# Spacing the shuffles of two blocks' quotients, and moving four small VectorE instructions behind the features of block 1

## The chip, the cores and the metric

The kernel runs on one core of a Trainium2 chip. The core has five engines that work side by side, each through its own instruction queue in order: TensorE (PE in the profile; PEld is its loading of weights), VectorE (DVE), ScalarE (ACT), GpSimd (POOL) and SyncE (SP), which here only issues DMAs. The metric is the device time of the whole launch in microseconds; lower is better. Engines wait for each other through semaphores. SBUF is the on-chip memory that all engines read and write, PSUM the eight banks into which TensorE multiplies.

## The reference

One input `x` of 2048 tokens by 640 numbers is normalized, and two layers run on the normalized tokens side by side: linear attention with a learned feature map (32 heads of 20 numbers), and an MLP of 1728 hidden numbers with a normalization of its own.

```python
xn = _layernorm(x)
# attention
q, k, v = split(xn @ wqkv)                       # 32 heads of 20
phi(p) = concat(softmax(p @ w_phi), softmax(-p @ w_phi))
kv  = einsum("hsf,hsd->hfd", phi(k), v);  z = sum_s phi(k)
o   = einsum("hqf,hfd->hqd", phi(q), kv) / (einsum("hqf,hf->hq", phi(q), z) + 1e-6)
A   = o @ wo
# MLP
y   = _layernorm(xn)
B   = gelu(y @ w1 + b1) @ w2 + b2
out = x + A + B
```

Both normalizations start from the same mean and variance of a token, so the kernel computes two inverse deviations for each token from one variance: `ry`, by which the MLP's input is scaled, and `rs_all`, by which the exponentials of the attention's features are scaled.

## The kernel before

All matmuls are float32 made of parts: a number is split into a high and a low half (ScalarE writes the high half, VectorE or GpSimd subtracts it from the number to get the low one), and a product takes three matmuls (high by high, high by low, low by high; lines 70 to 72). The tokens are in four blocks of 512, b = 0 to 3. The stages, in order of time:

- To about 213 us: normalization, and the MLP of blocks 0 and 1. The hidden layer is cut in 14 pieces of 128, taken in pairs g = 0 to 6. `passes(g, b, ws)` multiplies two pieces, applies gelu, and multiplies back; VectorE adds each of the five results to `acc[b]` (L329 for g = 0, L331 later).
- To about 431 us: the attention's projections, softmax features, and the sums over keys, one tile of 128 tokens after the other.
- To about 640 us: the MLP of blocks 2 and 3. For g = 1 to 5 `cross` makes the first products of both blocks together, and `second` the products back (accumulated by L342). Between them runs `attend`, the attention's second half, for the four blocks in turn.
- To the end: the attention's output times `wo`, added to `acc`.

**Ticks.** After each product of three matmuls the program calls `mlp.tick()`. It first issues what is due at that tick (`mlp.after(n, step)` puts a step n ticks ahead), then takes one step of the generator `mlp.beside`. So work of the other engines is put between TensorE's products by hand. On VectorE, ScalarE and GpSimd the order of instructions is the order of the program (from L1357 on, and up to L872, by `manual_schedule`; TensorE's from L516 to the end); the order of SP's queue is not written by hand but made by a planner, which puts a DMA where it takes it to be ready.

**The start.** `stats` (L132) yields between its parts; its last part (L160 to L162) is a reciprocal of 128 x n numbers and a product of the same size, which give `rs_all`. Three such generators stand for tokens 0 to 255 (`s01`), 256 to 511 (`s23`) and 512 to 1023 (`s47`). `next_y` (L653) is the `beside` of the first two passes: it runs what is left of gelu for block 0 (`zs`), splits the last weights (`parts`), and makes the MLP's input of block 1 in five chunks: GpSimd subtracts the mean (L679), VectorE multiplies (L681), ScalarE writes the high half (L683), VectorE the low one (L685). L671 turns the feature weights once.

**The attention's second half.** `Attention.groups` loads the features `e` eleven times for a block, splits them (`first`: ScalarE L1206, GpSimd L1207) and multiplies (`second`: L1213, L1214, into one of two banks); ScalarE moves one half of the result (L1223), and two ticks later VectorE adds the other (L1227) into the block's tile `ob`. There are two such tiles: block 2 uses that of block 0, block 3 that of block 1 (L1165). A group takes four ticks; a block takes 50.

When a block's groups are through, its `quotients` (L1234) run: denominators go to DRAM and come back with 128 of them in a row (`dt`), VectorE inverts them (L1246), they go to DRAM again, and five DMAs bring them to `rx`. Then, for each of five chunks, VectorE spreads the inverses over the partitions (`stream_shuffle`, L1262), GpSimd multiplies (L1264), and for blocks 0 and 1 a DMA stores the chunk to `ob_dram` (L1266), since another block takes the tile. `load_ob` (L1386) brings blocks 0 and 1 back before the last stage, with one DMA of 1280 KB each (L1388). `attend` (L1313) steps the groups and all quotients that have begun, one step of each for a tick.

Of the kernel before, what the change touches and what calls it, by code (L numbers as in the profile page):

```python
# [46 lines left out]
def f(ap):  # L47
    return ap.bitcast(F32)
# [3 lines left out]
def tile_kernel(ctx: ExitStack, tc: tile.TileContext, x, xT, wkT, wqT, wv, wphi, wo, w1, b1, w2, b2,  # L52
# [79 lines left out]
    def stats(ts, xp, xbs, turned=False, eng=nc.vector):  # L132

        t0, n = ts[0], len(ts)
        st = xp.tile([P, n, 2, 6], F32, name="st", bufs=2)
        for i, (t, xb) in enumerate(zip(ts, xbs)):
            for h in range(2):
                nc.vector.bn_stats(st[:, i, h, :], xb[:, h * 320:(h + 1) * 320])  # L138
            nc.vector.bn_aggr(mv[:, t, :], st[:, i, :, :])
            yield  # L140


        ts = slice(t0, t0 + n)
        q = xp.tile([P, 2, n], F32, name="q", bufs=2)
        eng.tensor_scalar(q[:, 1, :], mv[:, ts, 1], 0.25 * (1 + EPS), 0.25 * EPS * EPS, op0=ALU.mult, op1=ALU.add)
        eng.tensor_scalar(q[:, 0, :], mv[:, ts, 1], 0.25, 0.25 * EPS, op0=ALU.mult, op1=ALU.add)
        yield

        sr = xp.tile([P, 2, n], F32, name="sr", bufs=2)
        rr = xp.tile([P, 2, n], F32, name="rr", bufs=2)  # L150
        nc.scalar.activation(sr, q, AF.Sqrt)
        nc.vector.reciprocal(rr, sr)
        nc.vector.tensor_tensor(rr, rr, q, op=ALU.mult)
        if turned:
            nc.vector.scalar_tensor_tensor(sr, sr, -1.0, rr, op0=ALU.mult, op1=ALU.subtract)
        else:
            nc.vector.tensor_tensor(sr, sr, rr, op=ALU.add)
        nc.vector.reciprocal(ry[:, ts], sr[:, 1, :])
        yield
        ra = xp.tile([P, n], F32, name="ra", bufs=2)  # L160
        nc.vector.reciprocal(ra, sr[:, 0, :])
        nc.vector.tensor_tensor(rs_all[:, ts], sr[:, 1, :], ra, op=ALU.mult)  # L162
# [41 lines left out]
    def load_rows(b, i=5):  # L204

        mr = mtile(i)
        loads[b] = nc.sync.dma_start(mr.rearrange("p a t -> p (a t)"),
                          (r_dram[1][0] if b == 1 else r_dram[2][b - 2]).rearrange("r t -> (r t)").unsqueeze(0).to_broadcast([P, 8 * P])).ins
        return mr
# [309 lines left out]
    def finish(p):  # L519
        for _ in p:  # L520
            pass
# [46 lines left out]
    s01, s23, s47 = (stats(range(a, b), xp, xbs, b < 8, nc.gpsimd if a == 2 else nc.vector) for a, b, xbs in ((0, 2, x0[:2]), (2, 4, x0[2:]), (4, 8, x1)))  # L568

    def step(gen, n):  # L570
        for _ in range(n):
            next(gen, None)
# [56 lines left out]
    def raws(batch):  # L629
        ts = []  # L630
        for us in batch:
            raw = fp.tile([P, D], F32, name="raw")
            for n, g, u, nu, i in by_group(us):
                r, kk = g * G6, G6 if g < 5 else 2 * DH
                for j, one in enumerate(n):
                    with tc.issue_after(loads[1]) :
                        nc.sync.dma_start(raw[j * kk:(j + 1) * kk, u * P:(u + nu) * P],
                                          {"k": wkT, "q": wqT}[one][r:r + kk, i.start * P:i.stop * P])
            ts.append(raw)
        return ts  # L640
# [12 lines left out]
    def next_y():  # L653

        for _ in range(3):
            yield
        next(rows1)
        for z in zs[:2]:
            z()
        finish(rows1)  # L660
        mr = load_rows(1)
        first_raws.extend(raws(jobs[0]))
        for z in zs[2:]:
            z()
        for c in range(2, 4):
            parts[c][1]()
        for st in (s23, s47):
            step(st, 1)
        for _ in range(4):
            yield  # L670
        nc.vector.tensor_tensor(wpt[:, :, :, 1:], wpt[:, :, :, 1:], wpt[:, :, :, 0:1].to_broadcast([G6, 6, 6, DF]), op=ALU.subtract)  # L671
        for _ in range(9):
            yield
        xcs = {}
        for n in range(2 * KC + 5):
            c, i = divmod(n, 2)
            if i == 0 and c < KC:
                xcs[c] = xp.tile([P, D], F32, name="xb")[:, :512]
                nc.gpsimd.tensor_tensor(xcs[c], acc[1][:, c], mr[:, 0], op=ALU.subtract)  # L679
            if i == 0 and 0 <= (d := c - 1) < KC:  # L680
                nc.vector.tensor_tensor(xcs[d], xcs[d], mr[:, 1], op=ALU.mult)  # L681
            if i == 1 and 0 <= (d := c - 1) < KC:
                nc.scalar.activation(y[1][0][:, d], xcs[d], AF.Copy)  # L683
            if i == 0 and 0 <= (d := c - 2) < KC:
                nc.vector.tensor_tensor(y[1][1][:, d], xcs[d], f(y[1][0][:, d]), op=ALU.subtract)  # L685
            yield

    mlp.beside = next_y()
    p10 = mlp.passes(1, 0, [wc[2], wc[3]])
    next(p10)  # L690
# [470 lines left out]
    class Attention:  # L1161
# [72 lines left out]
        def quotients(self):  # L1234

            den, rden = d_dram[self.b]
            ob, parts = self.ob, [(slice(0, 20), "(q c) t -> q c t", 4), (slice(20, 30), "(q c) t -> q c t", 2)]
            for i, (r, form, q) in enumerate(parts):
                nc.sync.dma_start(den[r].rearrange(form, q=q), ob[30 + i::128 // q])
            dt = ep.tile([P, P], F32, name="dt")  # L1240
            nc.sync.dma_start(dt, den.rearrange("h (q t) -> (h q) t", q=4))
            for i in range(2):
                nc.sync.dma_start(ob[30 + i::32], o_dram[self.b].rearrange("(q i c) t -> i q c t", i=2, c=KC)[i])
            for i in range(13):
                yield
            nc.vector.reciprocal(dt, dt)  # L1246
            nc.sync.dma_start(rden.rearrange("h (q t) -> (h q) t", q=4), dt)
            for i in range(6):
                yield

            nc.sync.dma_start(rx[0::32], rden[0:20].rearrange(parts[0][1], q=4))
            yield
            for o in (0, 32):
                nc.sync.dma_start(rx[o + 1::64], rden[20:30].rearrange(parts[1][1], q=2))
                yield
                nc.sync.dma_start(rx[o + 2::64], rden[30:32].unsqueeze(1).to_broadcast([2, KC, 512]))
                yield
            for i in range(12):
                yield
            for c in range(KC + 1):  # L1260
                if c < KC:
                    nc.vector.stream_shuffle(rx[:, c, :], rx[:, c, :], SPREAD)  # L1262
                if c:
                    nc.gpsimd.tensor_tensor(ob[:, c - 1, :], ob[:, c - 1, :], rx[:, c - 1, :], op=ALU.mult)  # L1264
                    if self.b < 2:
                        nc.sync.dma_start(ob_dram[self.b][:, c - 1], ob[:, c - 1])  # L1266
                for i in range(3):
                    yield

        def split(self, c, eng):  # L1270
# [137 lines left out]
    step = 0  # L1408
# [79 lines left out]
```

## Time and profile before

| | us |
|---|---|
| median of 3 runs | 712.24 |
| lowest and highest of them | 711.95, 714.44 |
| the profiled execution | 711.95 |
| its span in the profile | 710.2 |
| TensorE busy | 703.4 |
| VectorE busy | 514.5 |
| GpSimd busy | 421.7 |
| ScalarE busy | 341.5 |

The profile is of one execution. Its span runs from the first to the last instruction; the launch takes 1.75 us more. A row of the timeline has start, duration (both in us), engine, line, operation, what is written and read, shapes, and a count; in brackets the engine's idle time before it and who ended it. Rows of SPq are issues of DMAs: their time is that of the issue, not of the transfer. A row of the waits has who waited, for whom, the sum in us, how often, and the longest. A row of the stretches has the stretch, its length, then busy time (and count) of PE, PEld, DVE, ACT and POOL, TensorE's granted clock, the share of the DMA engines and GB/s.

### The profile page before, as it was taken

What the parts mean: (1) busy time and instruction counts of PE and PEld (TensorE: products, weight loads), DVE (VectorE), ACT (ScalarE), POOL (GpSimd) and SP (SyncE); (2) the same over time, 40 slices, a digit from 0 to 9 for tenths busy, and PEclk for the clock granted to TensorE, in tenths of its full rate; (3) what the DMA queues carried; (4) which work ended last, traced back from release to release, by engine and by line L of the source; (5) the groups of instructions that cost most, each with busy time, mean ns of one, the idle gap of its engine ahead of it and who ended that gap; (6) DMA issues with size and microseconds to landing.
All of it is one profiled execution on the core that took longest, in us unless ns stands there. A gap on an engine that the chain in (4) does not pass through costs nothing.

```text
span 710.2 us, 9748 instructions
## 1 busy us (share of the span) xinstructions
PE 703.4 (99%) x3381; PEld 591.9 (83%) x3381; DVE 514.5 (72%) x819; ACT 341.5 (48%) x563; POOL 421.7 (59%) x362
## 2 busy tenths in 40 slices
PE   9999999999999999999999999999999999999998
PEld 7788888888888888888888888888888878888886
DVE  7977755978754788788888878757769686884622
ACT  6534554344334545544544547367666766450100
POOL 3621314577245997898787879458679887540400
PEclk9999999999999999999999999999999999999999
DMA  9823643485621227336401608963455568436222
GB/s 327 271 90 114 191 119 97 156 264 176 214 105 74 93 75 238 78 105 200 104 0 25 167 0 335 226 209 112 124 163 155 169 188 315 147 125 214 86 78 74
DMA packets 65767, 106.56 MB, mean 150 GB/s; under 512 B 7462, under 2 KB 31814, under 8 KB 63838
## 3 DMA queue, kind: packets, MB, share of 16 engines
q1 hardware_dynamic: 65414, 105.93, 46.7%
q8 instruction: 26, 0.43, 0.3%
q14 instruction: 23, 0.19, 0.1%
q10 hardware_dynamic: 304, 0.01, 0.0%
HBM read 71.37 MB, written 34.55 MB: 149 GB/s over the span
## 4 chain that ended last, share of the span: by engine, by line
PE 94%; DVE 3%; DMA 1%; ACT 1%; issue 0%; SPq 0%; DVEq 0%
PE bank L905 28%; PE bank L70 19%; PE bank L72 18%; PE bank L71 18%; PE bank L975 3%; PE bank L646 2%; PE bank L1213 1%; PE bank L1214 1%; DMA xb<-in_x 1%; DVE st L138 1%; DMA r<-sr 1%; PE bank L326 1%; PE bank L308 1%; PE bank L327 1%; PE bank L307 1%; PE bank L1145 1%
## 5 line engine op out<-in xcount | busy, mean ns | idle before, releaser
L905 PE MATMUL bank<-wkh,y 128*128 128x512 f32 (+1 forms) x480 | 139.5, 364 | 0.0
L70 PE MATMUL bank<-y,w 128*128 128x512 f32 (+1 forms) x294 | 114.3, 389 | 0.0
L71 PE MATMUL bank<-y,w 128*128 128x512 f32 (+1 forms) x294 | 113.7, 387 | 0.0
L72 PE MATMUL bank<-y,w 128*128 128x512 f32 (+1 forms) x294 | 113.6, 387 | 0.0
L64 POOL TENSOR_TENSOR w<-r,w 128x640 fp32r<-128x640 f32 x32 | 52.2, 1647 | 91.7 <-ACT w L61 62.2
L70 PE MATMUL bank<-m,w 128*128 128x512 f32 x260 | 102.4, 394 | 1.2 <-DVE acc L329 1.0
L72 PE MATMUL bank<-m,w 128*128 128x512 f32 x260 | 101.3, 390 | 0.0
L71 PE MATMUL bank<-m,w 128*128 128x512 f32 x260 | 101.2, 389 | 0.0
L905 PEld LDWEIGHTS bank<-wkh,y 128*128 128x128 f32 x480 | 87.5, 188 | 13.3
L905 PE MATMUL bank<-wkl,y 128*128 128x512 f32 (+1 forms) x240 | 87.4, 364 | 0.0
L70 PEld LDWEIGHTS bank<-y,w 128*128 128x128 f32 x294 | 55.2, 188 | 11.6 <-issue 0.4
L72 PEld LDWEIGHTS bank<-y,w 128*128 128x128 f32 x294 | 55.2, 188 | 11.3
L71 PEld LDWEIGHTS bank<-y,w 128*128 128x128 f32 x294 | 55.3, 188 | 11.0
L941 ACT ACTIVATE m<-m,rs_all 128x1280 f32<-128x1280 f32 x32 | 43.7, 1366 | 42.9 <-POOL m L940 42.8
L70 PEld LDWEIGHTS bank<-m,w 128*128 128x128 f32 x260 | 48.9, 188 | 12.1 <-DVE acc L329 1.5
L943 DVE TENSOR_REDUCE sm<-m 128x64 f32<-128x1280 f32 x32 | 47.4, 1482 | 14.9 <-ACT m L941 14.8
L905 PE MATMUL bank<-w,y 128*128 128x512 f32 x240 | 57.4, 391 | 0.0
L72 PEld LDWEIGHTS bank<-m,w 128*128 128x128 f32 x260 | 48.8, 188 | 10.3
L71 PEld LDWEIGHTS bank<-m,w 128*128 128x128 f32 x260 | 48.8, 188 | 9.9 <-DVE m L461 0.2
L940 POOL TENSOR_TENSOR m<-m,mx 128x640 f32<-128x640 f32 (+2 forms) x48 | 44.4, 938 | 19.3 <-DVE mx L929 19.3
L331 DVE TENSOR_TENSOR acc<-bank,acc 128x512 f32<-128x512 f32 x70 | 46.9, 683 | 10.9 <-PE bank L72 5.8
L905 PEld LDWEIGHTS bank<-w,y 128*128 128x128 f32 x240 | 44.4, 188 | 8.5
(186 smaller groups left out, 1447.2 us busy)
## 6 DMA issues: line engine op xcount, KB each, us to landing
r<-in_w SPq DMA_DIRECT2D x52, 320.0 KB
e<-e SPq DMA_DIRECT2D x40, 256.0 KB
e<-acc SPq DMA_DIRECT2D x52, 160.0 KB
acc<-in_xT SPq DMA_DIRECT2D x4, 1280.0 KB
t<-t SPq DMA_DIRECT2D x8, 512.0 KB
tf<-t SPq DMA_DIRECT2D x2, 1536.0 KB
xb<-in_x SPq DMA_DIRECT2D x8, 320.0 KB
t<-in_x SPq DMA_DIRECT2D x8, 320.0 KB
```

The costliest lines, as they stand in the source:

```text
L64: eng.tensor_tensor(lo, src, f(hi), op=ALU.subtract)
L70: nc.tensor.matmul(ps, lh, rh, start=first, stop=False, **kw)
L71: nc.tensor.matmul(ps, lh, rl, start=False, stop=False, **kw)
L72: nc.tensor.matmul(ps, ll, rh, start=False, stop=last, **kw)
L138: nc.vector.bn_stats(st[:, i, h, :], xb[:, h * 320:(h + 1) * 320])
L331: nc.vector.tensor_tensor(acc[b][:, m, :], pw, acc[b][:, m, :], op=ALU.add)
L646: nc.tensor.matmul(ps[:, u * nh * DF:(u + 1) * nh * DF], raw[:nh * DH, u * P:(u + 1) * P], wpt[:nh * DH, g, :nh, 1:], start=True, stop=True)
L905: nc.tensor.matmul(ps, lh[:, kc, c], rh[:, kc], start=n == 0, stop=n == 3 * KC - 1)
L940: subs[n, t] = nc.gpsimd.tensor_tensor(ep[:, s], a, b, op=ALU.subtract)
L941: exps[n, t] = nc.scalar.activation(e, e, AF.Exp, scale=rs_all[:, t:t + 1])
L943: nc.vector.tensor_reduce(sm, e.rearrange("p s (h f) -> p (s h) f", f=DH), axis=AX, op=ALU.add)
L975: nc.tensor.matmul(kvp[g // 2][:, (g % 2) * 240:(g % 2) * 240 + 240].rearrange("p (s f) -> p s f", s=4), v[:, g * VS:(g + 1) * VS], ft[:, ...
```

## The change

It has two parts. In `next_y` the last part of `s23` and `s47` (two reciprocals and two products of VectorE) is no longer issued ahead of block 1's features, but after them, each followed by a yield. In `quotients` the loop over chunks yields four times instead of three for each chunk of blocks 0 and 1; blocks 2 and 3 keep three.

```diff
@@ -664,8 +664,6 @@
             z()
         for c in range(2, 4):
             parts[c][1]()
-        for st in (s23, s47):
-            step(st, 1)
         for _ in range(4):
             yield
         nc.vector.tensor_tensor(wpt[:, :, :, 1:], wpt[:, :, :, 1:], wpt[:, :, :, 0:1].to_broadcast([G6, 6, 6, DF]), op=ALU.subtract)
@@ -683,6 +681,9 @@
                 nc.scalar.activation(y[1][0][:, d], xcs[d], AF.Copy)
             if i == 0 and 0 <= (d := c - 2) < KC:
                 nc.vector.tensor_tensor(y[1][1][:, d], xcs[d], f(y[1][0][:, d]), op=ALU.subtract)
+            yield
+        for st in (s23, s47):
+            step(st, 1)
             yield
 
     mlp.beside = next_y()
@@ -1264,7 +1265,7 @@
                     nc.gpsimd.tensor_tensor(ob[:, c - 1, :], ob[:, c - 1, :], rx[:, c - 1, :], op=ALU.mult)
                     if self.b < 2:
                         nc.sync.dma_start(ob_dram[self.b][:, c - 1], ob[:, c - 1])
-                for i in range(3):
+                for i in range(4 if self.b < 2 else 3):
                     yield
```

## The prediction

> **What bounds the kernel now.** I read the page first, then who waited for whom on TensorE, then the timeline around each of the waits found.
>
> ```profile
> span 710.2 us, 9748 instructions
> PE 703.4 (99%) x3381; PEld 591.9 (83%) x3381; DVE 514.5 (72%) x819; ACT 341.5 (48%) x563; POOL 421.7 (59%) x362
> ...
> PE bank L579 <- POOL m L577: 1.3, 1, 1.3
> PE bank L70 <- DVE acc L329: 1.0, 1, 1.0
> PE bank L1213 <- DVE acc L1227: 0.6, 1, 0.6
> ```
>
> TensorE is busy for 703.4 of 710.2 us. The change adds and removes no matmul, so it can only move TensorE's waits. The first (1.3 us) is the warm-up at the start, which the change doesn't touch. The other two are where a part of the change stands: DVE's accumulation L329 comes late at 31 us, and DVE's L1227 at 578 us. Together they bound the gain at about 2 us; all of the rest is a question of new waits.
>
> **The change, first part: the inverse deviations.** Two RECIPROCAL (L161) and two TENSOR_TENSOR (L162) leave DVE's queue ahead of block 1's features.
>
> ```profile
> 25.95 1.33 DVE L162 TENSOR_TENSOR rs_all<-sr,ra 128x2 f32<-128x2 f32 x1
> 27.41 1.41 DVE L162 TENSOR_TENSOR rs_all<-sr,ra 128x4 f32<-128x4 f32 x1
> 28.74 0.68 DVE L64 TENSOR_TENSOR m<-m,m 128x512 fp32r<-128x512 f32 x1
> ...
> 30.72 0.74 DVE L329 SCALAR_TENSOR_TENSOR acc<-bank,b2t,acc 128x512 f32<-128x512 f32 x1
> ...
> 25.64 3.15 POOL L64 TENSOR_TENSOR w<-r,w 128x640 fp32r<-128x640 f32 x2 [0.75 <-ACT w L61]
> ...
> 26.80 0.63 ACT L61 ACTIVATE m<-m 128x512 fp32r<-128x512 f32 x1
> ...
> 30.09 0.39 PE L72 MATMUL bank<-m,w 128*128 128x512 f32 x1
> 31.51 0.50 PE L70 MATMUL bank<-m,w 128*128 128x512 f32 x1 [1.04 <-DVE acc L329]
> ```
>
> TensorE's loss is 31.51 - 30.09 - 0.23 (its usual step between matmuls, three in each 0.68 us) = 1.19 us. The removed work looks like 2.9 us of DVE, since L64 could start when ACT has written its half, at 26.80 + 0.63 = 27.43, not at 28.74. But a product of 128x2 numbers cannot cost 1.33 us of arithmetic. Its two records end at 27.28 and 28.82, and GpSimd's pair of L64 runs from 25.64 to 28.79, with its middle at 27.2. So DVE's instruction, which reads both inputs from SBUF, sat out a GpSimd instruction each time. L64 on DVE has two SBUF inputs as well. If it is issued at 27.43, GpSimd's second instruction is 0.2 us old, and L64 does its work after 28.79. What a blocked one needs after the release is seen here:
>
> ```profile
> 571.84 1.14 DVE L461 TENSOR_TENSOR m<-m,m 128x512 fp32r<-128x512 f32 x1
> ...
> 570.86 1.57 POOL L393 TENSOR_TENSOR w<-r,w 128x640 fp32r<-128x640 f32 x1
> ```
>
> GpSimd ends at 572.43, DVE at 572.98: 0.55 us later. So L64 ends at 28.79 + 0.55 = 29.34, where it now ends at 29.42. Everything behind it (L671, another L64, L329) follows by the same amount: **a gain of 0.07 us**. The bounds are 0 and 1.19 us (L64 runs at once, and the wait goes); I take 0.07, because both records of L162 and the pair quoted here end where GpSimd lets them.
>
> [...]
>
> The four moved instructions come after the last accumulation of that pass, in this gap, with GpSimd without any work:
>
> ```profile
> 48.09 0.69 DVE L64 TENSOR_TENSOR m<-m,m 128x512 fp32r<-128x512 f32 x1 [2.13 <-ACT m L61]
> ...
> 40.00:60.00 20.00, 20.00 (x101) 16.95 (x101) 11.50 (x19) 10.60 (x18) 0.00 (x0) 1.00 0.11 32
> ```
>
> Without GpSimd beside them they need some 0.6 us of the 2.13 us that DVE waits for ACT. Their result is read only by the exponentials after 213 us. They issue no DMA. Cost 0; were the gap filled, L64 at 48.09 would end 0.6 us later, and no more than that could reach TensorE.
>
> **Second part: shuffles of blocks 0 and 1.** I number ticks (one for each product of three matmuls) from block 1's first shuffle. By the loops, its shuffles now stand at ticks 0, 3, 6, 9, 12 and the GpSimd multiplications at 3, 6, 9, 12, 15. They come to 0, 4, 8, 12, 16 and 4, 8, 12, 16, 20. The wait at 578 us:
>
> ```profile
> 576.27 0.74 DVE L1262 STREAM_SHUFFLE rx<-rx 128x512 f32<-128x512 f32 x1
> 576.90 0.67 DVE L342 TENSOR_TENSOR acc<-bank,acc 128x512 f32<-128x512 f32 x1
> 577.50 0.69 DVE L461 TENSOR_TENSOR m<-m,m 128x512 fp32r<-128x512 f32 x1
> 578.11 0.67 DVE L1227 TENSOR_TENSOR acc<-bank,ts 64x512 f32<-64x512 f32 x1
> ...
> 576.33 1.30 POOL L1264 TENSOR_TENSOR acc<-acc,rx 128x512 f32<-128x512 f32 x1
> ...
> 577.83 0.39 PE L72 MATMUL bank<-y,w 128*128 128x512 f32 x1
> 578.84 0.50 PE L1213 MATMUL bank<-m,kvs 128*128 128x512 f32 x1 [0.62 <-DVE acc L1227]
> ```
>
> TensorE loses 578.84 - 577.83 - 0.23 = 0.78 us to L1227. The second shuffle (576.27) moves behind L1227, so L342 starts at 576.27 and L461 is issued near 576.9. GpSimd's first multiplication is now due at tick 4, still ahead of everything else in its queue, so it starts at 576.33 as before and ends at 577.63. L461 reads two inputs from SBUF; it waits for that end and finishes at 577.63 + 0.55 = 578.18, which is where it ends now (577.50 + 0.69 = 578.19). L1227 then starts at 578.11, unchanged: **a gain of 0**. The bounds are 0 and 0.78 us; I take 0 because L461's present end fits the blocked form to 0.01 us. From 578 to 583 us the count of instructions ahead of each accumulation stays equal, and the last shuffle goes to a stretch where DVE waits for TensorE.
>
> Block 0's five shuffles, 50 ticks earlier, lie where TensorE waits for nothing. Its last store moves back too, and block 2's first write to that tile waits for it near 556 us; the idle stretch behind it takes up a delay of 2 us.
>
> ```profile
> 561.78 0.69 DVE L452 TENSOR_TENSOR m<-bank,m 128x512 f32<-128x512 f32 x1 [2.61 <-PE bank L72]
> ```
>
> So I cost block 0 at 0; if that cover were gone, it would cost what block 1 does below.
>
> What is late next is GpSimd's last multiplication (tick 20, not 15), its store, and whoever waits for the store. Block 3's attention writes its sums over block 1's tile, so its first DVE write (L1227 at 596.45) waits for that store; and `load_ob(1)` reads what it wrote.
>
> ```profile
> 588.21 1.28 POOL L1264 TENSOR_TENSOR acc<-acc,rx 128x512 f32<-128x512 f32 x1
> ...
> 592.24 1.29 POOL L1207 TENSOR_TENSOR e<-e,m 128x512 fp32r<-128x512 f32 x1
> ...
> 591.05 0.39 SPq L1266 DMA_DIRECT2D ob<-acc  x1
> 592.65 0.33 SPq L1388 DMA_DIRECT2D tf<-ob  x1
> 593.03 0.65 SPq L1175 DMA_DIRECT2D e<-e  x1
> 593.74 0.63 SPq L356 DMA_DIRECT2D r<-in_w  x1
> 595.10 0.32 SPq L1388 DMA_DIRECT2D tf<-ob  x1
> ...
> 598.64 0.32 SPq L1295 DMA_DIRECT2D w<-woh  x1
> 599.40 1.84 SPq L1175 DMA_DIRECT2D e<-e  x2
> ...
> SPq L1388 <- DMA ob<-acc: 0.6, 1, 0.6
> SPq L1295 <- DMA tf<-ob: 1.5, 1, 1.5
> SPq L1175 <- DMA e<-e: 0.4, 1, 0.4
> ...
> 596.45 0.68 DVE L1227 TENSOR_TENSOR acc<-bank,ts 64x512 f32<-64x512 f32 x1
> 597.05 0.67 DVE L342 TENSOR_TENSOR acc<-bank,acc 128x512 f32<-128x512 f32 x1
> ...
> 599.60 0.39 PE L70 MATMUL bank<-m,w 128*128 128x512 f32 x1
> ```
>
> Now the last multiplication runs at 588.21, its store is issued at 591.05, and it has landed when the second L1388 stops waiting, at 595.10. DVE needs it at 596.45: 1.35 us to spare. Afterwards the fourth multiplication has the slot at 588.21, and the last one that at 592.24 (after L1207 and L393, which are due at tick 19): it ends at 593.53, four microseconds later. SP's queue is put in order by a planner (only the other four engines are ordered by hand), by when it thinks each DMA ready. Its present order has L393's follower L356 behind the 1280 KB load of 592.65 and the `e` load of 593.03; a store that follows L393 on GpSimd should come behind all three. The load then takes the store's place at 591.05. It needs 598.64 - 592.65 = 5.99 us, so it lands at 597.04. The `e` load behind it now lands by 599.40, 0.76 us after the load: 256 KB cost 0.76 us there. So: `e` 597.8, the 160 KB of L356 598.3, the store 599.0. DVE then does L1227 and L342 (597.72 - 596.45 = 1.27 us) by 600.3. L342 empties the bank (three in turn) into which TensorE wants to write at 599.60: **a loss of 0.67 us**.
>
> The bounds: the store stays ahead of the load, is issued at 593.5, takes 4.05 us as now and lands at 597.6; 1.27 us more is 598.9, and TensorE loses 0. Or the load isn't earlier (598.64) and the next `e` load gets ahead too: 598.64 + 0.76 + 0.48 + 0.76 + 0.76 = 601.4, a loss of 3.07 us. I take 0.67, nearest to the present order of the queue.
>
> [...]
>
> **The sum.** The profiled execution took 711.95 us, 1.75 us more than its span; the median of the three runs is 712.24 us, 0.29 us above it. 711.95 - 0.07 - 0 + 0.67 = 712.55; on the median's scale **712.8 us**.
>
> **Rivals.**
> - *The order of SP holds.* The store keeps ahead of the load, and both old waits stay: 712.24 - 0.07 = 712.2 us. For it: the planner may see the multiplication earlier than the chip does.
> - *The waits go.* DVE gets at SBUF before GpSimd does, and the instructions taken away count in full: 1.19 or 0.78 us or both, 711.5 to 710.3 us. For it: on paper DVE is rid of 2.9 us and 0.63 us just ahead of each wait. Against it: both ends fit GpSimd's.
> - *Slower.* The store falls behind a second 1280 KB load as well (L1295, 598.64 now). At 0.76 us for 256 KB that load is worth 3.8 us; the store lands at 601.4 + 3.8 = 605.2, DVE stands still from 596.4, and TensorE loses 605.2 + 1.27 - 599.6 = 6.9 us: 719.1 us. A landing costs TensorE something from 598.3 on, and over 0.5% from 602.0 on. Against it: L1295 stands eight DMAs behind the first L1388 now, and the multiplication is done by 593.53.
> - *It doesn't do what its name says.* The loop yields three times now, four times after; a distance of three and four ticks, not four and five. The sum uses the loop, so nothing changes in it.
>
> **How the numbers follow.** Forecast 0.43, order holds 0.26, waits go 0.21, slower rival 0.07, else 0.03. The range reaches from both waits gone (710.27) to the upper bound of the loss (712.24 - 0.07 + 3.07 = 715.2): 710.2 to 715.2. A measurement tells about 0.5% (3.6 us) from no change. Faster by that needs more than both waits, 0.02; slower needs the last rival, 0.09; within it 0.89.
>
> **What would show it.** L64 on DVE at 27.4 us, blocked until 28.8, and TensorE's wait for L329 still about 1 us; L461 ending 0.55 us after a GpSimd multiplication near 577.6, and the wait for L1227 still there; the last L1266 behind the first L1388 on SP, and DVE's first L1227 into block 3's tile some 2.5 us later than 596.45, with a new TensorE wait for L342 near 600 us. It is wrong if the two old waits shrink by more than 0.3 us together, or if the store stands ahead of the load, or if TensorE waits more than 3 us at any new place.

## The result, and the profile after

| | before | after |
|---|---|---|
| median of 6 runs each, us | 712.90 | 716.78 |
| lowest and highest, us | 711.95, 714.93 | 715.97, 717.32 |
| the profiled execution, us | 711.95 | 715.97 |
| its span, us | 710.2 | 714.2 |

The ratio is 1.0050, with an interval of 1.0034 to 1.0065: 3.9 us more by these medians. The forecast was 712.8, 0.6 us above the median that it started from, with a range that ended at 715.2. In the new kernel the numbers of L669 to L685 are smaller by two, and those behind them larger by one (L1265 is the multiplication, L1267 the store, L1389 the load back, L1228 the sum).

The first line of the new page, then who waited for whom on TensorE (us in all, how often, the longest):

```profile
span 714.2 us, 9747 instructions
```

```profile
PE bank L70 <- DVE acc L342: 2.2, 1, 2.2
PE bank L579 <- POOL m L577: 1.3, 1, 1.3
PE bank L70 <- DVE acc L329: 1.0, 1, 1.0
PE bank L1214 <- DVE acc L1228: 0.6, 1, 0.6
```

The two old waits, for L329 and for L1228 (L1227 before), are still there, and on top stands a new one, for L342. Its place is near 600 us. The timeline of the new kernel there, for SP, GpSimd, VectorE and TensorE:

```profile
590.07 0.39 SPq L1267 DMA_DIRECT2D ob<-acc  x1
590.50 0.43 SPq L1389 DMA_DIRECT2D tf<-ob  x1
591.29 0.32 SPq L1176 DMA_DIRECT2D e<-e  x1
592.02 1.30 POOL L1265 TENSOR_TENSOR acc<-acc,rx 128x512 f32<-128x512 f32 x1
592.10 0.71 SPq L356 DMA_DIRECT2D r<-in_w  x1
593.35 0.54 SPq L1267 DMA_DIRECT2D ob<-acc  x1
...
598.53 0.32 SPq L1296 DMA_DIRECT2D w<-woh  x1
599.26 0.39 PE L72 MATMUL bank<-m,w 128*128 128x512 f32 x1
600.46 0.32 SPq L1389 DMA_DIRECT2D tf<-ob  x1
600.52 0.68 DVE L1228 TENSOR_TENSOR acc<-bank,ts 64x512 f32<-64x512 f32 x1 [4.13 <-DMA ob<-acc]
601.12 0.67 DVE L342 TENSOR_TENSOR acc<-bank,acc 128x512 f32<-128x512 f32 x1
601.85 0.50 PE L70 MATMUL bank<-m,w 128*128 128x512 f32 x1 [2.21 <-DVE acc L342]
603.00 0.63 PE L1215 MATMUL bank<-e,kvs 128*128 128x512 f32 x1
605.99 0.48 PE L70 MATMUL bank<-m,w 128*128 128x512 f32 x1
```

Read it in the order of cause. The last multiplication of block 1 runs at 592.02. Its store (593.35) has four SP issues ahead of it: the fourth chunk's store, the 1280 KB load of 590.50, an `e` load and L356. The load has landed when L1296, which waits for it, is issued at 598.53; the store, when the second L1389 is, at 600.46. VectorE's L1228 starts then, after 4.13 us of standing still. L342 behind it frees the bank, and TensorE goes on at 601.85, having stood for 601.85 - 599.26 - 0.23 = 2.36 us.

That is only part of the 4.0 us by which the spans differ. The stretches around it have the rest (their columns: busy time of PE, PEld, DVE, ACT, POOL, then TensorE's granted clock, the share of the DMA engines, GB/s):

```profile
592.00:599.00 7.00, 7.00 (x32) 5.82 (x31) 4.33 (x5) 4.09 (x7) 5.13 (x5) 1.00 0.94 310
...
603.00:606.00 3.00, 3.00 (x9) 2.31 (x8) 2.44 (x4) 2.98 (x7) 2.25 (x2) 0.50 1.03 429
```

In the 7 us ahead the granted clock is 1.00. In the 3 us from 603 on TensorE is busy throughout, at a granted clock of 0.50: from 603.00 to 605.99 its matmuls start in seven steps of 0.427 us, not 0.227. That is 7 x 0.20 = 1.4 us, and 1.6 us with the longer step on each side (0.33 and 0.32 us). So 2.36 + 1.6 = 4.0 us, all of it here, in the profiled execution; what the other runs say of the 1.6 us is told further down.

### The profile page after: what moved, and what is told of

Read it like the earlier page. It is cut to its first block, busy times and chain, and to the rows that moved or that the text cites. A ratio compares the mean times of both kernels' runs of the same rounds, so it can differ in the third digit from the quotient of the medians.

```text
span 714.2 us, 9747 instructions
## 1 busy us (share of the span) xinstructions
PE 705.1 (99%) x3381; PEld 593.2 (83%) x3381; DVE 515.9 (72%) x819; ACT 341.6 (48%) x563; POOL 421.8 (59%) x362
## 4 chain that ended last, share of the span: by engine, by line
PE 92%; DVE 4%; DMA 1%; ACT 1%; POOL 1%; issue 1%; ACTq 0%; DVEq 0%; POOLq 0%
PE bank L906 28%; PE bank L70 18%; PE bank L72 18%; PE bank L71 18%; PE bank L976 3%; PE bank L646 2%; PE bank L1214 1%; PE bank L1215 1%; DMA ob<-acc 1%; DVE st L138 1%; PE bank L327 1%; PE bank L308 1%; PE bank L326 1%; PE bank L307 1%; PE bank L1146 1%
## 5 line engine op out<-in xcount | busy, mean ns | idle before, releaser
L64 POOL TENSOR_TENSOR w<-r,w 128x640 fp32r<-128x640 f32 x32 | 52.3, 1648 | 93.1 <-ACT w L61 62.2
L331 DVE TENSOR_TENSOR acc<-bank,acc 128x512 f32<-128x512 f32 x70 | 46.9, 683 | 10.6 <-PE bank L72 5.4
L64 DVE TENSOR_TENSOR m<-m,m 128x512 fp32r<-128x512 f32 (+1 forms) x34 | 27.9, 828 | 34.1 <-ACT m L61 34.0
```

Of the source, the lines that this page charges most:

```text
L64: eng.tensor_tensor(lo, src, f(hi), op=ALU.subtract)
L331: nc.vector.tensor_tensor(acc[b][:, m, :], pw, acc[b][:, m, :], op=ALU.add)
```

## The experiments

Theory: everything is lost at block 1's last store, which lands late because the 1280 KB load got ahead of it on SP; TensorE stands still for that, and its clock falls because it stood still. The first part of the change and block 0's half of the second do nothing. Rivals: the part moved to 46 us or block 0 costs something; the late multiplication, not the place in the queue, makes the store late; the half clock has another source.

**One part alone, three times.** The first part without the spacing:

```diff
-                for i in range(4 if self.b < 2 else 3):
+                for i in range(3):
```

> Only the first part of the change: the four small VectorE instructions stand behind block 1's features, the shuffles as before. Theory (the whole loss comes from block 1's last store, which lands behind the 1280 KB load): no loss, the time of the kernel before less 0.06 us, TensorE's wait for L329 still 1.0 us, L64 on VectorE issued near 27.4 us and done near 29.3 us. Rival (moving the four instructions disturbs what comes after them): over 1 us slower than before.

Then the spacing of block 0 alone, and of block 1 alone, both without the first part (`if self.b == 0`, `if self.b == 1`):

> Only block 0's shuffles are four ticks apart. Theory: within 0.3 us of before; block 0's last store moves back too, but VectorE's idle time near 560 us takes it up, no new wait of TensorE. Rival (the wider spacing costs by itself, whichever the block): about half of the loss, 2 us.

> Only block 1's shuffles are four ticks apart. Theory: the whole loss, 3.9 us slower than before (716.8 us on a base of 712.9), with TensorE's wait of 2.2 us for L342 near 600 us, the wait of 4.1 us of VectorE's first sum into block 3's tile for the store, and half the granted clock for 3 us after it. Rival (half and half by blocks): about 2 us slower.

| | median, us | ratio to before | interval |
|---|---|---|---|
| deviations moved, alone | 712.97 | 0.9996 | 0.9986 to 1.0006 |
| block 0 alone | 712.98 | 0.9994 | 0.9984 to 1.0003 |
| block 1 alone | 717.61 | 1.0056 | 1.0041 to 1.0071 |

The whole loss is block 1's. Who waited for whom on VectorE in the kernel with block 1 alone, from 585 to 612 us, and its stretch from 603 us:

```profile
DVE acc L1227 <- DMA ob<-acc: 4.4, 1, 4.4
```

```profile
603.00:606.00 3.00, 2.69 (x7) 2.14 (x8) 2.83 (x5) 2.12 (x4) 0.80 (x1) 0.58 1.02 408
```

The same wait for the store, and again the low clock after it.

**The store ahead of the load.** In the changed kernel, both loads back are held until block 1's last store is issued, so that only the place in the queue is undone:

```diff
-                        nc.sync.dma_start(ob_dram[self.b][:, c - 1], ob[:, c - 1])
+                        self.stored = nc.sync.dma_start(ob_dram[self.b][:, c - 1], ob[:, c - 1]).ins
...
-        nc.sync.dma_start(at[b].ob, ob_dram[b])
+        with tc.issue_after(at[1].stored):
+            nc.sync.dma_start(at[b].ob, ob_dram[b])
```

> The whole change, but the 1280 KB load of block 0's quotients is kept behind block 1's last store in SP's queue. GpSimd's last multiplication is as late as in the changed kernel (ends near 593.3 us). Theory (it is the place behind the load that makes the store late, not the multiplication): the store lands by about 597 us, no wait for L342 near 600 us, full clock throughout, 712.8 us. Rival (the late multiplication is enough): VectorE's wait for the store stays over 2 us and the time near 715 us or above.

712.75 us, ratio 0.9992 (0.9980 to 1.0004). Its timeline:

```profile
592.71 1.30 POOL L1265 TENSOR_TENSOR acc<-acc,rx 128x512 f32<-128x512 f32 x1
...
594.04 0.32 SPq L1267 DMA_DIRECT2D ob<-acc  x1
...
595.30 1.77 DVE L461 TENSOR_TENSOR m<-m,m 128x512 fp32r<-128x512 f32 x1
596.05 1.07 SPq L1390 DMA_DIRECT2D tf<-ob  x2
...
596.99 0.67 DVE L1228 TENSOR_TENSOR acc<-bank,ts 64x512 f32<-64x512 f32 x1
```

The multiplication is as late as in the changed kernel, and the store is issued 0.7 us later than there. But both loads are behind it, VectorE takes up L1228 right behind L461, and the wait for L342 and the half clock are gone. So the place in the queue is the cause, not the late multiplication.

**Four chunks ahead, one behind.** The changed kernel, with 1024 KB of the load left where they were and the last 256 KB held until the store is issued:

```diff
-        nc.sync.dma_start(at[b].ob, ob_dram[b])
+        if b:
+            nc.sync.dma_start(at[b].ob, ob_dram[b])
+        else:
+            nc.sync.dma_start(at[b].ob[:, :4], ob_dram[b][:, :4])
+            with tc.issue_after(at[1].stored):
+                nc.sync.dma_start(at[b].ob[:, 4], ob_dram[b][:, 4])
```

> The changed kernel, in which block 0's load back is two DMAs: four of its five chunks (1024 KB) where the 1280 KB load stood, the fifth (256 KB) behind block 1's last store. Theory (the store waits for the bytes ahead of it in the queue, at the 8.0 us for 1280 KB that the changed kernel shows, 1.6 us for 256 KB): the store lands 1.6 us earlier than 600.45, at about 598.85; VectorE's first write into block 3's tile and L342 end 1.6 us earlier, TensorE's wait for L342 is 2.36 - 1.6 = 0.8 us, too short for the clock to fall, and the time is that of the run with the store ahead of the load plus 0.8, 713.5 us, the ratio 1.001. Rival A (the half clock follows any new wait at this place): 0.8 + 1.6, 715.1 us. Rival B (the landing hangs on the store's own issue and the traffic as a whole, not on the bytes ahead of it): landing at 600.4 again, 716.8 us.

714.52 us, ratio 1.0033 (1.0014 to 1.0053): between the theory's time and rival A's. Its timeline on SP, VectorE and TensorE, and the stretch from 603 us:

```profile
594.77 0.32 SPq L1267 DMA_DIRECT2D ob<-acc  x1
...
597.95 0.32 SPq L1394 DMA_DIRECT2D tf<-ob  x1
...
599.53 0.39 PE L72 MATMUL bank<-m,w 128*128 128x512 f32 x1
599.95 0.32 SPq L1390 DMA_DIRECT2D tf<-ob  x1
600.01 0.68 DVE L1228 TENSOR_TENSOR acc<-bank,ts 64x512 f32<-64x512 f32 x1 [3.01 <-DMA ob<-acc]
...
601.34 0.50 PE L70 MATMUL bank<-m,w 128*128 128x512 f32 x1 [1.42 <-DVE acc L342]
```

```profile
603.00:606.00 3.00, 3.00 (x14) 2.46 (x14) 2.77 (x5) 2.98 (x7) 2.76 (x2) 1.00 1.01 420
```

The 1024 KB have landed when L1394, which waits for them, is issued (597.95; the 1280 KB of the changed kernel at 598.53), and the store when L1390 is, at 599.95. That is 2.0 us behind the load, as in the changed kernel (600.46 - 598.53 = 1.93), and only 0.5 us earlier than there, not 1.6. So the price by bytes, 1.6 us for 256 KB, did not come out, and the landing lies nearer to rival B's 600.4 than to the theory's 598.85. But the store was issued 1.4 us later than in the changed kernel, since L356 ahead of it was (593.59, not 592.10), which the expectation had not reckoned with. So this run doesn't show what 256 KB ahead are worth, and it leaves rival B's account of the landing open. TensorE lost 601.34 - 599.53 - 0.23 = 1.58 us, not 0.8, and 0.49 us more in a second wait, for L1228 near 609 us, where VectorE was still behind. The clock stayed at 1.00: rival A falls, though its time was near.

**TensorE kept busy in the wait.** The changed kernel, with ten matmuls whose result nothing reads, ahead of the product that waits for L342:

```diff
+                if (g, b, m) == (5, 2, 1):
+                    spare = banks.tile([P, 512], F32, name="bank1")
+                    for _ in range(10):
+                        nc.tensor.matmul(spare, w[:, 0, ms], hid[0][0], start=True, stop=True)
```

> The changed kernel, with ten matmuls more (2.3 us of TensorE, their result is not read) just ahead of the product that waits for L342 near 600 us. Theory (the loss of 3.9 us is the wait, 2.4 us, and 1.6 us more because TensorE gets half the clock for some 3 us after standing still): the matmuls fill the wait, TensorE idles under 0.7 us there, the granted clock stays 1.0, 1.6 us faster than the changed kernel (715.2 us on its 716.8). Rival (half the clock has another cause, for instance the DMA traffic at that time): clock 0.5 again after the wait, same time as the changed kernel or longer.

716.63 us, ratio 1.0045 (1.0030 to 1.0061). Its timeline on TensorE, and the stretch from 603 us:

```profile
600.32 2.43 PE L342 MATMUL bank<-m,w 128*128 128x512 f32 x10
...
603.18 0.50 PE L70 MATMUL bank<-m,w 128*128 128x512 f32 x1 [0.43 <-DVE acc L346]
```

```profile
603.00:606.00 3.00, 2.82 (x12) 2.36 (x13) 2.94 (x6) 2.24 (x4) 0.92 (x1) 1.00 0.98 407
```

The store was as late as in the changed kernel, or later, but TensorE worked through most of the wait, and the clock stayed at 1.00. Over a whole run 3.4 us at half clock bring the mean granted clock to 0.998 (1 - 0.5 x 3.41 / 714.2), which the changed kernel's profile has. None of the four runs of this kernel shows that (0.999 to 1.000); three of the six runs of the changed kernel do, and three of the four with block 1 alone. So standing still is the likely source of the half clock; with so few runs it is not proved. The 1.6 us were not won: matmuls and wait took 2.9 us together, a wait of 0.5 us for the attention's sum near 610 us came in, and one of 0.8 us near 153 us. The last isn't this edit's doing: waits for L331 near 153 us come and go, 0.2 to 0.8 us in nine of the other profiles and none in four, those of before and after among them. By the medians 0.3 us of the loss is gone, which the interval can't tell from none.

**What holds the two old waits.** The prediction put both down to a VectorE instruction that sits out a GpSimd instruction. Six kernels tried to undo that from the kernel before. First the GpSimd instruction at 27 us (the split of piece 3's second weights) was put behind L671:

```diff
-        for c in range(2, 4):
-            parts[c][1]()
+        parts[2][1]()
...
         nc.vector.tensor_tensor(wpt[:, :, :, 1:], ...)
+        parts[3][1]()
```

> The kernel before with one edit: the split of the second weights of piece 3 (ScalarE, then GpSimd, 1.57 us) moves behind L671, four ticks later; the four small VectorE instructions stay where they were. Theory (GpSimd's instruction holds SBUF's shared inputs, and it is what makes L329 late): the second L162 takes about 0.2 us, not 1.41, L64 starts near 27.45 us and takes 0.68 us, TensorE's wait of 1.0 us for L329 is gone, 1.2 us faster (0.17%). Rival (VectorE's instructions ahead of L64 are the cause): L162 still over 1 us and the wait as it was.

712.99 us, ratio 0.9996 (0.9987 to 1.0005): no gain. Its timeline:

```profile
27.38 0.16 DVE L162 TENSOR_TENSOR rs_all<-sr,ra 128x4 f32<-128x4 f32 x1
27.46 0.69 DVE L64 TENSOR_TENSOR m<-m,m 128x512 fp32r<-128x512 f32 x1
27.96 1.62 POOL L64 TENSOR_TENSOR w<-r,w 128x640 fp32r<-128x640 f32 x1 [0.72 <-ACT w L61]
28.06 2.25 DVE L670 TENSOR_TENSOR wpt<-wpt 120x684 f32<-120x684 f32 x1
```

With no GpSimd instruction beside it, the second L162 takes 0.16 us where it took 1.41, and L64 runs at once. But the moved instruction starts at 27.96, as soon as ScalarE has its half, and L670 takes 2.25 us instead of 0.87. The wait only changed its victim.

Six ticks later is far enough:

```diff
-        for _ in range(9):
+        for _ in range(6):
+            yield
+        parts[3][1]()
+        for _ in range(3):
             yield
```

> The kernel before, in which the split of piece 3's second weights (ScalarE's copy and GpSimd's subtraction, one step) comes six ticks behind L671 instead of ahead of the deviations' last steps. Theory (GpSimd's pair of L64 holds SBUF while VectorE stands in front of it): with the second GpSimd instruction of the pair moved to about 32 us, L162 and L64 run at once, L329 is issued about 1.2 us earlier, TensorE's wait for L329 near 31.5 us goes, the time is 1.1 us less than before, 711.8, the ratio 0.9985. Rival (the moved GpSimd instruction blocks a later VectorE instruction, as it did when it came right behind L671): a wait of 0.5 to 1.2 us for another L329 between 32 and 37 us, 712.5 to 713. If piece 3's weights then come too late, TensorE waits for the GpSimd's L64 near 38 us.

712.38 us, ratio 0.9991 (0.9980 to 1.0003). Who waited for whom on TensorE there:

```profile
PE bank L70 <- DVE acc L331: 0.6, 2, 0.4
PE bank L1215 <- DVE acc L1229: 0.6, 1, 0.6
```

The wait for L329 is gone. By the starts of its matmuls TensorE now loses 0.44 us for L331 at 38 us (ahead of which L683 and L687 need 1.77 and 1.78 us beside GpSimd), 0.21 us at 153 us and 0.41 us at 193 us: 1.06 of the 1.19 us saved, and the span is 710.2 us, as before. But the last two come in other profiles as well (with the deviations moved alone, 0.60 and 0.36 us), and the first is missing from the last kernel of this section, which has the same edit. So that the edit only trades one wait for others is not shown; its median is 0.7 us below that of the kernel before, and the interval holds both no gain and the whole 1.1 us expected.

The sum at 578 us was to come one tick earlier, ahead of L461. The first try hit the wrong group (block 2's group 7, where the late one is 6), alone and together with the first of the two edits above:

> The kernel before with one edit: of block 2's attention, the eighth group's sum (L1227) is due one tick after its product, not two, which puts it ahead of L461 in VectorE's queue. Theory (L461, blocked by GpSimd's multiplication, holds up the sum that TensorE waits for): TensorE's wait of 0.6 us at 578 us is gone, 0.8 us faster (0.11%). Rival (the shuffles are the load that matters): the wait stays, since no shuffle moves.

> Both edits of the two runs before it, on the kernel before. Theory: both waits of TensorE gone, 2.0 us faster than before (0.28%), which would beat both kernels. Rival: a gain at one place is lost at the next wait, under 1 us.

712.60 us (0.9991, 0.9980 to 1.0002) and 713.23 us (0.9997, 0.9988 to 1.0005): both old waits still there, as they had to be. The second had a wait of 0.9 us at 550 us besides, again for an L461 stretched to 1.84 us beside GpSimd. With the right group:

```diff
-            mlp.after(2, whole)
+            mlp.after(1 if (self.b, g) == (2, 6) else 2, whole)
```

> The kernel before, in which one sum of the attention's groups is issued one tick earlier: that of block 2's group 6, whose L1227 is the one that TensorE waits for at 578 us (the run that moved group 7's left that wait as it was). Theory (the sum is late because L461, ahead of it on VectorE, sits out a GpSimd instruction that holds SBUF): ahead of L461 the sum reads PSUM and one SBUF tile, isn't blocked, and is done by about 577.6; TensorE's wait for L1227 near 578.8 goes, the time is 0.8 us less than before, 712.1, the ratio 0.999. Rival (L461, now behind the sum, is late for TensorE instead): a wait for the weights of L461 takes its place, and the time is 712.9. Second rival (the sum waits for ScalarE's copy L1223 when it is one tick early): the wait is 0.3 to 0.6 us as before.

713.87 us, ratio 1.0014 (1.0004 to 1.0023). Its timeline:

```profile
576.96 0.67 DVE L1227 TENSOR_TENSOR acc<-bank,ts 64x512 f32<-64x512 f32 x1
...
578.29 1.77 POOL L1207 TENSOR_TENSOR e<-e,ph 128x512 fp32r<-128x512 f32 x1
...
578.79 1.81 DVE L461 TENSOR_TENSOR m<-m,m 128x512 fp32r<-128x512 f32 x1
...
582.63 0.50 PE L1213 MATMUL bank<-ph,kvs 128*128 128x512 f32 x1 [1.22 <-DVE acc L1227]
```

The sum is done by 577.63, over 1 us earlier than it was, and the wait at 578 us is gone. L461, later now, runs into the next GpSimd instruction, needs 1.81 us, and makes the next group's sum late: 582.63 - 581.02 - 0.23 = 1.38 us lost (the matmul ahead starts at 581.02) where it was 0.78. Both edits together:

> Both edits: piece 3's split six ticks behind L671, and block 2's group 6 summed one tick earlier. Theory: the two gains are at different places and add up, 1.1 + 0.8 = 1.9 us less than before, 711.0, the ratio 0.9973, TensorE waiting for neither L329 nor L1227. Rival (one of the two moves its wait elsewhere): 711.8 to 712.2. Second rival (both do): 712.9.

713.42 us, ratio 1.0004 (0.9990 to 1.0018). No wait for L329, the longer one for the sum, waits of 0.9 us in all for L331. None of these kernels beats the one before by more than can be measured.

## Why the prediction was wrong

**First part, the deviations: right.** The timeline after, at the three places named:

```profile
25.55 3.17 POOL L64 TENSOR_TENSOR w<-r,w 128x640 fp32r<-128x640 f32 x2 [0.75 <-ACT w L61]
27.37 1.90 DVE L64 TENSOR_TENSOR m<-m,m 128x512 fp32r<-128x512 f32 x1 [1.62 <-ACT m L61]
...
31.37 0.51 PE L70 MATMUL bank<-m,w 128*128 128x512 f32 x1 [0.98 <-DVE acc L329]
...
46.24 0.17 DVE L162 TENSOR_TENSOR rs_all<-sr,ra 128x4 f32<-128x4 f32 x1
48.14 0.69 DVE L64 TENSOR_TENSOR m<-m,m 128x512 fp32r<-128x512 f32 x1 [1.73 <-ACT m L61]
```

L64 is issued when its input is there and ends at 29.27, 0.55 us after GpSimd; 29.34 was forecast. The matmul ahead of the wait starts at 30.01, so TensorE loses 1.13 us instead of 1.19: a gain of 0.06, with 0.07 forecast. The four moved instructions end at 46.41 and leave VectorE 1.73 us of idle time.

**Shuffles, the wait at 578 us: right.**

```profile
576.19 1.29 POOL L1265 TENSOR_TENSOR acc<-acc,rx 128x512 f32<-128x512 f32 x1
576.70 1.33 DVE L461 TENSOR_TENSOR m<-m,m 128x512 fp32r<-128x512 f32 x1
```

GpSimd ends at 577.48, L461 0.55 us later, at 578.03, and the wait stands. Block 0 cost nothing (ratio 0.9994), as forecast.

**Block 1's last store: the chain was right, its size wrong.** The slot of the multiplication (end 593.53 forecast, 593.32 measured), the place behind the load, the `e` load and L356, the wait of VectorE and that of TensorE for L342 all came as described. The step that failed is "It needs 5.99 us, so it lands at 597.04". That was the duration of a load that started after a quieter moment and with less beside it. In the kernel before and then in the one after, the 2 us ahead of its issue, and the time from its issue to its landing, read:

```profile
590.65:592.65 2.00, 2.00 (x11) 1.65 (x10) 0.49 (x1) 1.12 (x2) 2.00 (x3) 1.00 0.61 194
592.65:598.64 5.99, 5.99 (x28) 4.98 (x27) 4.88 (x9) 4.05 (x7) 3.42 (x3) 1.00 0.87 301
```

```profile
588.50:590.50 2.00, 2.00 (x11) 1.65 (x10) 0.32 (x1) 0.60 (x1) 2.00 (x2) 1.00 0.94 335
590.50:598.53 8.03, 8.03 (x37) 6.67 (x36) 4.33 (x5) 4.79 (x8) 6.63 (x6) 1.00 0.99 310
```

Brought forward by 2 us, the load starts 0.43 us behind a 256 KB store and shares the DMA engines with all that was there: 598.53 - 590.50 = 8.0 us, landing 1.5 us later than forecast. They moved as much per microsecond as before (310 and 301 GB/s), but 2.5 MB until the load had landed, not 1.8 MB, and 1.3 MB of either are the load. What comes behind the load was sized rightly: 1.96 us to the store's landing forecast, 1.93 measured. With TensorE 0.1 us earlier at its own place, 0.67 us became 2.36. The bound of 3.07 us was wide enough for that; the value taken was that of a quieter queue. How much of the 2.0 us each neighbour in the queue takes was not separated.

**The half clock: missing.** The sentence "so it can only move TensorE's waits" left out that the same matmuls can get slower (0.427 us apart, not 0.227); no term, no bound and no rival held it. In the profiled execution it is 1.6 of the 4.0 us. It is not in every run: of the six runs of the new kernel, three have a mean granted clock of 0.998, as it would leave, and took 715.97 to 716.72 us; the other three have 1.000 and took 716.84 to 717.32 us, no less. (With block 1 alone the one run at 1.000 was the shortest, 716.24 us against 717.38 to 718.11.) So the profile shows 1.7 us more than forecast for the late store (2.36 for 0.67) and 1.6 us for the half clock; what takes the place of the latter in the runs without it stays open. A part may be the second wait of 0.5 us near 609 or 610 us, which both profiles of a late store at full clock have and the changed kernel's has not. The start of the sum was low as well: 712.24 us, the median of three runs, against 712.90 of six, which is 0.7 of the 1.6 us by which the time left the range.

A landing at 600.5 already came with 0.5%; the forecast had 602.0 for that, and gave a slower result only to a second large load ahead of the store, which did not come (L1296 is issued five microseconds behind it). The range's upper end carried the whole of one mechanism, and nothing of what may follow a wait of its length.

**The other rivals.** The order of SP didn't hold. That the waits go was the rival with 0.21; in the new kernel both stayed. Of the attempts to remove them by hand, the first place tried for the GpSimd instruction kept the wait at 31 us and the second removed it, without a gain that can be measured; the one at 578 us only moved on.

## What to carry to other kernels

A DMA that gets ahead in a queue must be priced at its new start, with the traffic it meets there (8.03 us here, not 5.99), and with what stands behind it in that queue (the store landed 1.9 to 2.4 us after the load in all four kernels that had the load ahead); here one tick more per chunk put a 256 KB store behind 1280 KB. Where a planner orders a queue, work made late on another engine can change that order, and holding the large load until the small store is issued costs nothing measurable (712.75 us with it). A wait of 2.36 us on an otherwise full TensorE was followed in the profiled execution by 3.41 us at half clock, so a bound on such a wait should carry that too (here up to 1.6 us).

## What the runs showed of the hardware

**The clock fell after waits of 2.36 and 2.70 us.** TensorE stood still for 2.36 us in the changed kernel and 2.70 us with block 1 alone. The changed kernel's trace has a granted clock of 0.50 from 602.76 to 606.17 us, 3.41 us long, and 1.00 on both sides; its matmuls were 0.427 us apart there. With block 1 alone the clock was 0.58 in the 3 us from 603 and 0.93 in the 6 us behind them. The fall did not come with the wait, but 0.91 us after TensorE had gone on (602.76 - 601.85). After 1.58 us (four chunks ahead) the clock was 1.00 in the 3 us from 603, after 1.13 us (the changed kernel, at 31 us) the matmuls came 0.23 to 0.24 us apart from the second one on, and with 1.38 us (the right group) the mean granted clock of the profile was 0.999, where that of the changed kernel was 0.998. What a wait between 1.58 and 2.36 us does, no trace here shows.

Beside the half clock of 3.413 us, the clock record of the changed kernel's trace has stretches at full clock of 597.33 and 109.23 us, that of the kernel before one of 703.15 us: 175, 32 and 206 times 3.413 us, to within 0.07 us. Why three runs of the changed kernel stayed at 1.000 is not shown: no trace is of one of them.

**A VectorE instruction that sat out one of GpSimd's ended 0.55 us after it,** in the changed kernel at 29 us (29.27, GpSimd at 28.72) and at 578 us (578.03, GpSimd at 577.48) alike, and a product of 128x4 numbers took 1.41 us beside GpSimd (the kernel before) and 0.16 us without it (the split later). Moving either of the two mostly moved the collision: L670 was hit in place of L64, and L461 again one GpSimd instruction later.
